# Turning the row maxima on TensorE: an ordinary product on 24 columns in place of the transpose mode on 128

## The chip, the cores and the metric

The kernel runs on one core of a Trainium2 chip. The metric is the device time of one execution in microseconds (us); lower is better. A core has a matrix engine (TensorE, "PE" in the profile, its weight loads "PEld"), a vector engine (VectorE, "DVE"), a scalar engine (ScalarE, "ACT"), a general engine (GpSimd, "POOL") and a queue engine (SyncE, "SP") that issues most DMAs.

## The reference

Two independent halves of the output, side by side. The left one is a causal attention with a memory over four segments, the right one a Fourier mixing of another input:

```python
B, S, D = x.shape                       # 1, 2048, 576
H = 32; Dh = D // H; N = 4; L = S // N  # heads of 18, segments of 512
...
for s in range(N):
    qs, ks, vs = q[:, :, s], k[:, :, s], v[:, :, s]
    logits = jnp.einsum("bhqd,bhkd->bhqk", qs, ks) * scale + mask
    p = _softmax(logits, axis=-1)
    a_dot = jnp.einsum("bhqk,bhkd->bhqd", p, vs)
    pq = phi(qs)
    num = jnp.einsum("bhld,bhde->bhle", pq, M)
    den = jnp.einsum("bhld,bhd->bhl", pq, z)[..., None] + 1e-6
    o = g * (num / den) + (1.0 - g) * a_dot
    ...
    M = M + jnp.einsum("bhld,bhle->bhde", phi(ks), vs)
    z = z + jnp.einsum("bhld->bhd", phi(ks))
return o @ wo
...
a = jnp.einsum("bsd,ed->bse", x, dft_hid_re)
b = jnp.einsum("bsd,ed->bse", x, dft_hid_im)
y = jnp.einsum("ts,bse->bte", dft_seq_re, a) - jnp.einsum("ts,bse->bte", dft_seq_im, b)
```

All inputs and the output are float32.

## The kernel before

The kernel writes the order of every engine's instructions out by hand. It has three stages. In the first, up to some 220 us, the projections are computed segment by segment, with the sums of the memory (`accumulate`, L363) and the look-ups in it. In the second, up to some 930 us, two streams are woven together: the dense products of the Fourier half (`hidden`, L622 to L627, and `sequence` over `product`, L577) and the attention. A loop over 64 steps and a tail (`attention`) issues the attention in eight slots a step; between the slots a generator (`dense`) fills in dense products in proportion to planned costs. The third stage is the product with `wo` (L84).

The attention works on groups `G` of four heads of one segment, 32 groups in all; a step takes two heads. Their softmax needs each query's largest logit. For the "even" two heads of a group it goes this way:

- `s_fill` computes scores with queries on partitions (`scores`, L738, into PSUM banks of tag `s`) and takes each row's minimum of the negated scores on VectorE (`smallest`, L744) into `NEGM`, eight columns: two heads by four blocks of 128 queries.
- `maxima` (L788 to L791, GpSimd) cuts these eight float32 columns into three bfloat16 parts each, 24 columns of the tile `mb`. There are two such tiles, and their other columns are zero from two memsets (L483) that run once, at the beginning of the second stage.
- `maxima_transpose` turns them: the 24 columns become 24 rows of 128 queries. TensorE does it in transpose mode on all 128 columns (L795), into a free part of the PSUM bank that the score product L815 has just filled (tag `t`). ScalarE copies 24 rows out (L797, tile `mt`), and two DMAs on SyncE's queue put them as three more rows under the queries in `qs`.
- One step later `t_fill` computes the scores a second time, with keys on partitions and with these three rows in the contraction (L812, L815, L820, L821), so that the maximum is already taken off. ScalarE takes the exponentials out of the bank (L824, L825).

The turn's place in the order is fixed: it follows L815 in `t_fill(n, 1)` of every even step, directly ahead of dense products or, three times, of score products. Only for group 0, where no `t_fill` runs yet, does it have a bank of its own (`trm`). Each bank is used again once the engine that reads it is done.

TensorE's weight loads and products are separate records in the profile. A product names its operands as `out<-moving,stationary`. An f32 product here carries its own load; a bf16 one has an instruction of its own for it.

Of the kernel before, what the change touches and what calls it, by code (L numbers as in the profile page):

```python
# [15 lines left out]
BF16 = mybir.dt.bfloat16  # L16
AF = mybir.ActivationFunctionType
# [6 lines left out]
P = 128  # L24
# [16 lines left out]
def infini_attention_and_fnet(ctx: ExitStack, tc: tile.TileContext, xT, wqk, w8, wv, wo, beta, xtT, cT, hT, out):  # L41
    nc = tc.nc
    act, dve, pool, pe = nc.scalar, nc.vector, nc.gpsimd, nc.tensor
# [25 lines left out]
    ident16 = const.tile([P, P], BF16, name="ident16")  # L69
# [18 lines left out]
    def later(n, fn, *a):  # L88
        due.setdefault(clock[0] + n, []).append((fn, a))
# [112 lines left out]
    for i in range(2):  # L202
        kn.append(tuple(sk.tile([P, D], F32R, name=f"kn{n}{i}") for n in "hl"))
        t = sk.tile([P, 2, H, 19], F32R, name=f"vn{i}")
# [3 lines left out]
    for i in range(3):  # L208
        t = sb.tile([P, H, 55], BF16, name=f"vs{i}")
# [258 lines left out]
    CAUSAL, NEGM, MB, OG = [], [], [], []  # L468

    def attention_tiles():  # L470
        t = sr.tile([P, L], F32, name="causal")
        CAUSAL.append(t)
        for i in range(2):
            NEGM.append(sr.tile([P, 8], F32, name=f"negm{i}"))
            MB.append(sr.tile([P, P], BF16, name=f"mb{i}"))

    def attention_constants():
        t = CAUSAL[0]
        pool.memset(t, 0.0)
        pool.affine_select(t[:, 384:], t[:, 384:], pattern=[[-1, P]], base=0, channel_multiplier=1,  # L480
                           compare_op=OP.is_ge, fill=LOWEST)
        for m in MB:
            pool.memset(m, 0.0)  # L483

    NG = 32

# [13 lines left out]
    for s in range(NSEG):  # L500
# [8 lines left out]
        for n, m in enumerate((0, 1, 2, 3, 8, 4, 5, 6, 7)):  # L509
            project_qk(s, m)  # L510
            tick()
            if not more and n in (5, 7):
                h_split(0, (n - 5) // 2)
            if s and n < (8 if more else 4):
                copy_parts(s - 1, 2 * n)
                copy_parts(s - 1, 2 * n + 1)
            if s in (1, 2) and n >= 4:
                load_x(s + 1, n - 4)
            if not more and n == 0:
                for k in range(5):  # L520
                    h_load(0, k)
            if not more and n == 4:
                p1k.close()
                sr = ctx.enter_context(tc.tile_pool(name="sb2r", bufs=1, side="right", reuse_waits="tile"))
                attention_tiles()
            if not more and n == 4:
                c_load(0)
                c_load(1)
                stacks(sr, 0)
                stack_load(0)  # L530
            if not more and n == 6:
                c_load(2)
        for j in range(4):
            project_v(s, j, lookup(s, j) if s else iter(()))
            tick()
            for k in ((0, 1), (2, 3), (4,), ())[j] if s == 0 else ():
                load_x(1, k)
            if more and j in (1, 2):
                split_x(s + 1, j - 1)
            if not more and j == 1:  # L540
                stacks(sr, 1)
            if not more and j == 2:
                attention_constants()
            if not more and j == 0:
                h_split(0, 2)
                h_split(0, 3)
            if not more and j == 1:
                h_split(0, 4)
                c_cut(0, dve)
                c_cut(1, dve)  # L550
            if not more and j in (1, 3):
                c_load(3 + j // 2)
            if more and j:
                accumulate(j - 1)
# [228 lines left out]
        nc.sync.dma_start_transpose(PT[n], hl.rearrange("p a c -> p (a c)"))  # L783

    def maxima(G):
        m, b = NEGM[G % 2].rearrange("p (h n) -> p h n", h=2), MB[G % 2][:, :24].rearrange("p (h c n) -> p c h n", h=2, c=3)
        r = sa.tile([P, 2, 4], F32, name="negx", bufs=2)
        pool.tensor_copy(b[:, 0], m)  # L788
        pool.tensor_tensor(r, m, b[:, 0], OP.subtract)
        pool.tensor_copy(b[:, 1], r)  # L790
        pool.tensor_tensor(b[:, 2], r, b[:, 1], OP.subtract)  # L791

    def maxima_transpose(G, o):
        t = o[:, 384:448].bitcast(BF16)
        pe.transpose(t, MB[G % 2], ident16)  # L795
        w = sa.tile([24, P], BF16, name="mt", bufs=2)
        act.activation(w, t[:24], AF.Copy)  # L797
        for h in range(2):
            later(1, dma, qs_bufs[G % 4][NPAIR:NPAIR + 3, 2 * h].rearrange("c (n t) -> c n t", n=4), w[12 * h:12 * h + 12])

    def t_fill(n, kind, maxima_of=None):
        G, h = divmod(n, 4)
        q, k = qs_bufs[G % 4][:NPAIR + 3, h], ks_bufs[G % 4][:NPAIR + 3, h]
        if kind == 0:
            PT[n] = (sa.tile([P, 1280], F16, name="phi", bufs=2), sa.tile([P, 1280], F16, name="plo", bufs=2),
                     sa.tile([P, 1280], F32, name="pf", bufs=3))
        hi, lo, f = PT[n]
        o = bank("t", [P, L], F32, "t")
        if kind == 0:
            for j in range(4):  # L810
                b = slice(j * P, (j + 1) * P)
                pe.matmul(o[:, b], k[:, b], q[:, b], start=True, stop=True)  # L812
            r, w = 0, 512
        elif kind == 1:
            pe.matmul(o[:, :384], k[:, :128], q[:, 128:], start=True, stop=True)  # L815
            if maxima_of is not None:
                maxima_transpose(maxima_of, o)
            r, w = 512, 384
        else:
            pe.matmul(o[:, 256:384], k[:, 256:384], q[:, 384:], start=True, stop=True)  # L820
            pe.matmul(o[:, :256], k[:, 128:256], q[:, 256:], start=True, stop=True)  # L821
            r, w = 896, 384
        if kind:
            act.activation(hi[:, r:r + w], o[:, :w], AF.Exp, bias=LIFT, scale=SCALE)  # L824
        act.activation(f[:, r:r + w], o[:, :w], AF.Exp, bias=LIFT, scale=SCALE)  # L825
# [89 lines left out]
    def attention():  # L915
        for p in range(NP + V_LAG):
# [28 lines left out]
            if G is not None and p < T_LAG:  # L945
                maxima_transpose(G, bank("trm", [P, L], F32, "t"))
# [11 lines left out]
            if p % 2 and p < NP:  # L958
                maxima(p // 2)
# [28 lines left out]
    for w in attention():  # L988
        tick()
        ta += w  # L990
        while td / total_d < ta / total_a:
            t = next(d, BREAK)
# [14 lines left out]
    for t in range(NT):  # L1007
# [3 lines left out]
        for h in range(2):  # L1011
            cs = slice(h * 288, h * 288 + 288)
            o = ps.tile([P, 288], F32, name="d", bufs=3)
# [53 lines left out]
```

## Time and profile before

| | |
|---|---|
| median of three runs | 1001.27 us (1000.71 to 1001.88) |
| profiled execution | 1002.62 us, of which the span of the core's instructions is 1000.9 us |
| mean granted TensorE clock | 0.998 |
| busy share of the span | TensorE 99%, its loads 92%, VectorE 75%, ScalarE 71%, GpSimd 64% |
| turns of the maxima | 32 products of 221 ns and 32 loads of 98 ns in the records, 32 copies of 250 ns |

The times of the engines' parts are those of one profiled execution. TensorE's products overlap: a record's duration reaches from a product's start to its modelled end, and the next one starts long before it. What a product costs is therefore read from starts, not from durations.

### The profile page before, as it was taken

What the parts mean: (1) busy time and instruction counts of PE and PEld (TensorE: products, weight loads), DVE (VectorE), ACT (ScalarE), POOL (GpSimd) and SP (SyncE); (2) the same over time, 40 slices, a digit from 0 to 9 for tenths busy, and PEclk for the clock granted to TensorE, in tenths of its full rate; (3) what the DMA queues carried; (4) which work ended last, traced back from release to release, by engine and by line L of the source; (5) the groups of instructions that cost most, each with busy time, mean ns of one, the idle gap of its engine ahead of it and who ended that gap; (6) DMA issues with size and microseconds to landing.
All of it is one profiled execution on the core that took longest, in us unless ns stands there. A gap on an engine that the chain in (4) does not pass through costs nothing.

```text
span 1000.9 us, 25591 instructions
## 1 busy us (share of the span) xinstructions
PE 990.0 (99%) x9294; PEld 925.6 (92%) x9294; DVE 752.7 (75%) x2052; ACT 712.3 (71%) x1680; POOL 635.9 (64%) x700
## 2 busy tenths in 40 slices
PE   9999999989999999999999999999999999999998
PEld 8989989889999999999999999999999999999998
DVE  6557667594678777878898888898888899998321
ACT  7757575653887787878778788877767777777243
POOL 2657576675767667666766776776767767767000
PEclk9999999999999999999999999999999999999999
DMA  7537456767588999899999987889999999989455
GB/s 248 185 117 252 178 176 244 233 231 217 143 186 211 219 240 227 203 236 220 249 220 238 218 218 191 180 203 233 226 227 213 233 237 247 248 188 200 127 150 139
DMA packets 305614, 208.92 MB, mean 209 GB/s; under 512 B 206288, under 2 KB 260432, under 8 KB 305488
## 3 DMA queue, kind: packets, MB, share of 16 engines
q1 hardware_dynamic: 305248, 207.15, 81.0%
q8 instruction: 73, 1.20, 0.5%
q14 instruction: 53, 0.43, 0.2%
q10 hardware_dynamic: 240, 0.14, 0.0%
HBM read 121.32 MB, written 57.93 MB: 179 GB/s over the span
## 4 chain that ended last, share of the span: by engine, by line
PE 85%; DVE 5%; ACT 4%; issue 2%; POOL 1%; DMA 1%; SPq 0%; POOLq 0%; DVEq 0%; ACTq 0%
PE d L577 38%; PE s L738 7%; PE d L84 6%; PE v L84 4%; PE pv L856 4%; PE qk L250 4%; PE d L622 3%; PE d L623 3%; PE d L624 3%; PE pv L857 2%; PE m L363 1%; PE t L812 1%; PE qk L84 1%; DMA craw<-cT 1%; DVE r L276 1%
## 5 line engine op out<-in xcount | busy, mean ns | idle before, releaser
L744 DVE CUSTOM_DVE_ANT_0 s<-s,causal 128x128 f32<-128x128 f32 (+3 forms) x512 | 249.7, 498 | 103.2 <-PE s L738 94.1
L456 POOL TENSOR_TENSOR clo<-craw,chi 128x512 fp32r<-128x512 f32 x158 | 216.8, 1372 | 100.0 <-ACT chi L451 73.1
L577 PE MATMUL d<-wide,chi 128*128 128x288 f32 x1408 | 266.2, 306 | 0.4 <-DVE y L647 0.4
L577 PEld LDWEIGHTS d<-wide,chi 128*128 128x128 f32 x1408 | 211.8, 189 | 3.2 <-issue 0.9
L577 PE MATMUL d<-wide,clo 128*128 128x288 f32 x704 | 177.5, 319 | 0.0
L778 POOL TENSOR_TENSOR hl<-pf,hl 128x768 f16<-128x768 f32 x64 | 112.9, 1764 | 68.6 <-ACT hl L774 55.3
L824 ACT ACTIVATE phi<-t 128x384 f16<-128x384 f32 x128 | 61.7, 482 | 103.4 <-PE t L821 103.3
L738 PE MATMUL s<-ks,qs 108*128 108x128 bf16 (+3 forms) x512 | 133.9, 304 | 1.3 <-ACT pf L767 0.8
L767 ACT ACTIVATE pf<-s,nb 128x128 f32<-128x128 f32 (+3 forms) x256 | 128.3, 527 | 6.2
L839 DVE TENSOR_TENSOR plo<-pf,phi 128x384 f16<-128x384 f32 (+1 forms) x128 | 126.4, 987 | 0.0
L577 PE MATMUL d<-ab,chi 128*128 128x288 f32 x640 | 126.0, 306 | 0.0
L577 PEld LDWEIGHTS d<-wide,clo 128*128 128x128 f32 x704 | 118.6, 189 | 1.6
L825 ACT ACTIVATE pf<-t 128x384 f32<-128x384 f32 (+1 forms) x192 | 99.5, 518 | 6.1 <-PE t L812 5.9
L451 ACT ACTIVATE chi<-craw 128x512 fp32r<-128x512 f32 x160 | 100.1, 626 | 4.1 <-DMA craw<-cT 2.2
L577 PEld LDWEIGHTS d<-ab,chi 128*128 128x128 f32 x640 | 98.5, 189 | 0.6
L774 ACT ACTIVATE hl<-pf 128x768 f16<-128x768 f32 (+1 forms) x128 | 87.4, 729 | 2.0
L622 PE MATMUL d<-wide,chi 128*128 128x288 f32 x256 | 84.8, 331 | 2.8 <-ACT xtail L453 2.8
L577 PE MATMUL d<-ab,clo 128*128 128x288 f32 x320 | 84.8, 314 | 0.0
L623 PE MATMUL d<-wide,chi 128*128 128x288 f32 x256 | 76.1, 297 | 0.0
L624 PE MATMUL d<-wide,clo 128*128 128x288 f32 x256 | 76.0, 297 | 0.0
L778 DVE TENSOR_TENSOR hl<-pf,hl 128x512 f16<-128x512 f32 x64 | 67.7, 1058 | 0.1
L839 POOL TENSOR_TENSOR plo<-pf,phi 128x384 f16<-128x384 f32 x64 | 59.4, 928 | 12.9 <-ACT pf L825 10.3
(214 smaller groups left out, 2500.0 us busy)
## 6 DMA issues: line engine op xcount, KB each, us to landing
craw<-cT SPq DMA_DIRECT2D x128, 256.0 KB
ks<-kd SPq DMA_DIRECT2D x32, 432.0 KB
qs<-qd SPq DMA_DIRECT2D x32, 432.0 KB
craw<-xtT SPq DMA_DIRECT2D x32, 320.0 KB
vd<-vs SPq DMA_DIRECT2D x16, 440.0 KB
vst<-vd SPq DMA_DIRECT2D x32, 220.0 KB
qd<-p SPq DMA_DIRECT2D x16, 384.0 KB
kd<-p SPq DMA_DIRECT2D x16, 384.0 KB
```

The lines of the kernel that those rows point to most:

```text
L84: pe.matmul(o, a, b, start=n == 0, stop=n == len(terms) - 1)
L451: act.activation(hi, raw[:, :4], AF.Copy)
L456: engine.tensor_tensor(lo, raw[:, :4], hi.bitcast(F32), OP.subtract)
L577: pe.matmul(o[h], a, b[:, h * 288:h * 288 + 288], start=start, stop=stop)
L622: pe.matmul(o, xh[:, k], wl[k][:, cs], start=k == 0, stop=False)
L623: pe.matmul(o, xh[:, k], wh[k][:, cs], start=False, stop=False)
L624: pe.matmul(o, xl[:, k], wh[k][:, cs], start=False, stop=False)
L738: pe.matmul(o[:, c:c + w], q[:, i * P:w], k[:, :w], start=True, stop=True)
L744: dve.tensor_tensor_reduce(o[:, c:c + w], o[:, c:c + w], CAUSAL[0][:, L - w:], scale=scale, scalar=-LOWEST, op0=OP.add, op1=OP.min, accum_ ...
L767: act.activation(f[:, FIRST_COL[i]:FIRST_COL[i] + w], o[:, c:c + w], AF.Exp, bias=nb[:, i:i + 1], scale=-1.0)
L778: engine.tensor_tensor(hl[:, 1, a:b], f[:, a:b], hl[:, 0, a:b], OP.subtract)
L839: (pool if kind == 2 else dve).tensor_tensor(lo[:, a:b], f[:, a:b], hi[:, a:b], OP.subtract)
```

## The change

The tiles `mb` have 24 columns instead of 128, so nothing is left to be zeroed and the two memsets go. The turn is an ordinary product with `mb` as stationary operand (24 columns) and the bfloat16 identity as moving operand (128 columns); it writes 24 rows of float32 instead of 128 rows of bfloat16, and ScalarE's copy reads float32. The order of the instructions on every engine is otherwise the same. In the built program the new load and product are set to a part of the array of 128 rows by 32 columns.

```diff
-            MB.append(sr.tile([P, P], BF16, name=f"mb{i}"))
+            MB.append(sr.tile([P, 24], BF16, name=f"mb{i}"))
...
-        for m in MB:
-            pool.memset(m, 0.0)
...
     def maxima(G):
-        m, b = NEGM[G % 2].rearrange("p (h n) -> p h n", h=2), MB[G % 2][:, :24].rearrange("p (h c n) -> p c h n", h=2, c=3)
+        m, b = NEGM[G % 2].rearrange("p (h n) -> p h n", h=2), MB[G % 2].rearrange("p (h c n) -> p c h n", h=2, c=3)
...
     def maxima_transpose(G, o):
-        t = o[:, 384:448].bitcast(BF16)
-        pe.transpose(t, MB[G % 2], ident16)
+        t = o[:24, 384:512]
+        pe.matmul(t, MB[G % 2], ident16, start=True, stop=True)
         w = sa.tile([24, P], BF16, name="mt", bufs=2)
-        act.activation(w, t[:24], AF.Copy)
+        act.activation(w, t, AF.Copy)
```

## The prediction

> **What bounds the kernel now.** I read the page first: the busy times, then the chain that ended last.
>
> ```profile
> span 1000.9 us, 25591 instructions
> PE 990.0 (99%) x9294; PEld 925.6 (92%) x9294; DVE 752.7 (75%) x2052; ACT 712.3 (71%) x1680; POOL 635.9 (64%) x700
> PE 85%; DVE 5%; ACT 4%; issue 2%; POOL 1%; DMA 1%; SPq 0%; POOLq 0%; DVEq 0%; ACTq 0%
> ```
>
> TensorE has work in 990.0 of 1000.9 us and carries 85% of the chain. The second view is who TensorE waited for.
>
> ```profile
> PE d L622 <- ACT xtail L453: 2.8, 1, 2.8
> ...
> PE s L738 <- ACT pf L767: 0.8, 1, 0.8
> ```
>
> Its longest wait is 2.8 us, once, where the projections give way to the attention; the first wait inside the attention stage that the list shows is 0.8 us. So an edit in the attention stage is worth what it takes from or adds to TensorE's own stream of instructions, and little else. The third view is the two tiles that the change touches, `mb` and `mt`.
>
> ```profile
> L795 PEld LDWEIGHTS <-mb x32: 95/98/101, 243.5 to 898.6; 128*128 128x128 bf16 x32
> L795 PE MATMUL t<-ident,mb x31: 219/221/222, 265.9 to 898.8; 128*128 128x128 bf16 x31
> L797 ACT ACTIVATE mt<-t x31: 247/250/252, 268.2 to 900.5; 24x128 bf16<-24x128 bf16 x31
> ```
>
> There are 32 of these turns (31 on tile `t`, one on `trm`), one load, one product and one copy each. A duration of 221 ns is not what a product costs, because products overlap: what counts is by how much later the next ones start. So the fourth view is the timeline around one turn, and around a step of the same kind that has none.
>
> ```profile
> 265.72 0.33 PE L815 MATMUL t<-qs,ks 111*128 111x384 bf16 x1
> 265.88 0.22 PE L795 MATMUL t<-ident,mb 128*128 128x128 bf16 x1
> 265.91 0.38 PE L622 MATMUL d<-wide,chi 128*128 128x288 f32 x1
> 266.12 0.29 PE L623 MATMUL d<-wide,chi 128*128 128x288 f32 x1
> 266.25 0.30 PE L624 MATMUL d<-wide,clo 128*128 128x288 f32 x1
> ```
>
> ```profile
> 590.24 0.40 PE L812 MATMUL t<-qs,ks 111*128 111x128 bf16 x4
> 590.48 0.33 PE L815 MATMUL t<-qs,ks 111*128 111x384 bf16 x1
> 590.50 0.43 PE L626 MATMUL d<-wide,xtail 128*128 128x288 f32 x1
> 590.77 0.29 PE L627 MATMUL d<-wide,xtail 128*128 128x288 f32 x1
> 590.90 0.29 PE L622 MATMUL d<-wide,chi 128*128 128x288 f32 x1
> ```
>
> From the start of L815 to the start of the second dense product behind it (L623 above, L627 below) it is 266.12 - 265.72 = 0.40 us with a turn and 590.77 - 590.48 = 0.29 us without; one product further 0.53 against 0.42. A turn costs TensorE 0.11 us, and all 32 cost 3.5 us, 0.35% of the span. That is the most that the change could save on this engine.
>
> **The turn itself.** Why 0.11 us, when four products of the same 128 moving columns (L812) start 0.24 / 4 = 0.06 us apart? The weight loads tell.
>
> ```profile
> 265.72 0.10 PEld L795 LDWEIGHTS <-mb 128*128 128x128 bf16 x1
> 265.88 0.19 PEld L622 LDWEIGHTS d<-wide,chi 128*128 128x128 f32 x1
> 265.99 0.19 PEld L623 LDWEIGHTS d<-wide,chi 128*128 128x128 f32 x1
> ```
>
> The load of `mb` starts with L815 and lies under it, since L815 keeps the array for 265.88 - 265.72 = 0.16 us. The next load, the f32 one of the dense product, starts only with the turn's product at 265.88, and the one behind it follows after 0.11 us. So the 0.11 us are the time of an f32 load that has only a short product above it; the turn's own streaming is inside. (Behind 3 of the 32, by the order of the program, stands a bf16 load of a score instead; the argument is the same there.) The changed kernel keeps the 128 moving columns, the place in the order, and the f32 load behind. The load of 24 columns instead of 128 is shorter, but it was hidden. Hence the main term: 32 x (0.11 - 0.11) = 0. Its cover is L815; if the `mb` load could not run under it, it would cost one load step, taken as the 0.06 us of the L812 row, 32 x 0.06 = 1.9 us.
>
> What the trace lacks is a bf16 product with 24 stationary columns. In the built program it runs on a part of the array, 128 rows by 32 columns, where its neighbours use 128 by 128; the array is switched twice at each turn. The nearest rows are the sums of the memory (L363), whose last piece has 64 stationary columns and uses 128 by 64.
>
> ```profile
> L363 PEld LDWEIGHTS m<-vn,knh x72: 138/188/194, 42.9 to 174.9; 128*128 128x128 f32 x60, 128*64 128x64 f32 x12
> ```
>
> ```profile
> 61.25 0.19 PEld L363 LDWEIGHTS m<-vn,knh 128*128 128x128 f32 x1
> 61.36 0.14 PEld L363 LDWEIGHTS m<-vn,knh 128*64 128x64 f32 x1
> 61.43 0.19 PEld L250 LDWEIGHTS qk<-xh,wide 128*128 128x128 f32 x1
> 61.54 0.19 PEld L250 LDWEIGHTS qk<-xl,wide 128*128 128x128 f32 x1
> ```
>
> ```profile
> 61.43 0.23 PE L363 MATMUL m<-vn,knh 128*64 128x152 f32 x1
> 61.50 0.43 PE L250 MATMUL qk<-xh,wide 128*128 128x512 f32 x1
> ```
>
> Into the narrow piece the loads are 61.36 - 61.25 = 0.11 us apart, as between full f32 loads (61.54 - 61.43 = 0.11); out of it 61.43 - 61.36 = 0.07 us, less, since 64 columns load faster. The full load of L250 starts at 61.43, with the narrow product and not after its 0.23 us. Neither edge shows a stop. I take 0 for the switch. Bounds: below, the whole of today's 0.11 us saved; above, a stop at both edges, priced under the rivals.
>
> The Trainium skill, "TensorEngine Tiling (Array Packing)", section Tiling Modes, speaks against this: "Changing tiling mode (not just tile) drains the TensorE". The rows at 61.36 and 61.43 do not show it for 64 columns; no row here tries 32. The skill's "TensorE: Matmul & The Clock Gate", section on weight-path modes, also says that the fast weight load needs 128 columns, so the new load would lose it.
>
> **The wait that goes.** The old product wrote 128 rows of which the copy read 24; the new one writes 24. So 30 loads of later scores (L738) lose a wait for TensorE's own counter, met some 80 products earlier. One such place (521.35) and one without the wait (510.92):
>
> ```profile
> 521.35 0.39 PE L738 MATMUL s<-ks,qs 108*128 108x512 bf16 x1
> 521.39 0.62 PE L577 MATMUL d<-ab,chi 128*128 128x288 f32 x2
> ```
>
> ```profile
> 510.92 0.39 PE L738 MATMUL s<-ks,qs 108*128 108x512 bf16 x1
> 510.96 0.62 PE L577 MATMUL d<-wide,clo 128*128 128x288 f32 x2
> ```
>
> The next product follows after 0.04 us in both. Worth: 0.
>
> **The copy on ScalarE** reads 128 f32 elements a row instead of bf16. Bounds from f32 copies out of PSUM:
>
> ```profile
> L405 ACT ACTIVATE nd<-look 128x133 f32<-128x133 f32 x12 | 3.4, 286 | 0.0
> ...
> L406 ACT ACTIVATE nd<-look 128x76 f32<-128x76 f32 x12 | 3.0, 246 | 0.0
> ```
>
> ```profile
> ACT phi L824 <- PE t L821: 103.3, 61, 3.6
> ```
>
> Between 246 ns for 76 and 286 ns for 133 elements, 128 give about 283 ns, against 250 now: 32 x 0.033 = 1.1 us more on ScalarE. Behind it in that queue stand the exponentials (L824, L825), and behind those the bank that TensorE refills. ScalarE then waits for TensorE, 103.3 us in all at L824, so I take 0; if none of that slack lay behind it, 1.1 us. A gain of as much is possible only if the bf16 read is the slower, which these rows exclude.
>
> **The two memsets** of `mb` on GpSimd go. They stand ahead of the 2.8 us wait:
>
> ```profile
> 221.06 0.42 DVE L458 TENSOR_TENSOR xtail<-craw,xtail 64x128 fp32r<-64x128 f32 x1
> 221.29 0.35 POOL L483 MEMSET mb<- 128x128 bf16 x2
> ```
>
> ```profile
> 224.20:228.70 4.50, 4.50 (x23) 4.28 (x24) 2.62 (x10) 0.41 (x1) 4.36 (x4) 0.62 0.51 167
> ```
>
> GpSimd's later work waits for ScalarE anyway. VectorE's L458 ends at 221.48, 0.19 us after the first memset began; if the two disturb each other, at most 0.19 us goes from the chain to the wait. I take half, 0.1 us.
>
> **Sum.** 0 + 0 + 0 - 0.1 us. The profiled execution took 1002.62 us (span 1000.9) and would become 1002.5; it lies 1.35 us above the median of the three runs, 1001.27, so the forecast for the median is 1001.2. Three runs spread over 1.2 us, so about 0.2%, 2.0 us, is what a measurement of this kernel can tell from no change.
>
> **Rivals.**
>
> Slower, by the switch: the array empties before it changes its split. At entry alone the load waits for L815's end (0.33 us) and takes 0.10, so the turn starts 0.43 us after L815 instead of 0.16: +0.27 x 32 = 8.6 us, 1009.9. At the exit alone the f32 load waits for the turn's 0.22 us: +7.0 us, 1008.3. Both, 15.7 us, 1017. It decides as soon as the stop exceeds 0.06 us a turn. For it: the array really is split otherwise. Against: L363. Chance 0.12. The rule quoted above is this rival.
>
> A little slower: the load loses only its place under L815, +1.9 us, 1003.2. For it: a load of this form is new here. Against: 0.16 us of cover. Chance 0.08.
>
> Faster: the exposed f32 load gets earlier, and a turn costs its 0.06 us of streaming: 32 x 0.05 = 1.6 us, 999.7; at most 3.5 us, 997.8. For it: the new load leaves most columns alone. Against: at 61.43 the full load still starts with the narrow product. Chance 0.06.
>
> Faster, at the seam: after the 2.8 us wait TensorE's granted clock is 0.62 for 4.5 us, a loss of 4.5 x 0.38 = 1.7 us. A wait shorter by up to 0.19 us may escape it: 999.4. Against: most of the wait stays. Chance 0.04.
>
> **How the numbers follow.** No measurable change has 0.70. The range 999.0 to 1004.0 takes in that case with the spread of runs, ScalarE's 1.1 us, the small loss and the seam, together 0.82; it leaves out the stops and the larger gain. Faster by over 0.2%: most of the 0.06, and part of the seam, 0.08. Slower: the stops, half of the small loss, some scatter, 0.20. Same: 0.72.
>
> **What would show it.** Right: 0.40 us from L815 to the second dense product behind a turn, as now; the load of 24 columns still starting with L815; the copy at some 283 ns; the same chain. Wrong: that distance at 0.46 (the small loss), at 0.6 or more (a stop), or at 0.35 and less (the gain); or a granted clock of 1 behind the seam.

## The result: slower by 0.8%, and the profile after

| | before | after |
|---|---|---|
| median | 1001.27 us | 1009.19 us (1008.76 to 1009.38) |
| profiled execution / its span | 1002.62 / 1000.9 us | 1009.38 / 1007.6 us |
| ratio of the times, 95% interval | | 1.0079 [1.0068, 1.009] |

The change costs 7.9 us. The forecast of 1001.2 us and its range up to 1004.0 are wrong; the rival "slower, by the switch", given 0.12, is what happened.

First the page of the changed kernel: span, busy times and the chain that ended last.

```profile
span 1007.6 us, 25589 instructions
...
PE 997.5 (99%) x9294; PEld 925.9 (92%) x9294; DVE 756.3 (75%) x2052; ACT 712.3 (71%) x1680; POOL 635.9 (63%) x698
...
PE 88%; DVE 5%; ACT 4%; issue 1%; POOL 1%; DMA 0%; SPq 0%; DVEq 0%; POOLq 0%; ACTq 0%
```

The number of TensorE's products is the same, yet it is busy 997.5 - 990.0 = 7.5 us longer. The loads, ScalarE and GpSimd have not moved; VectorE is busy 3.6 us longer, with the same 5% of the chain. TensorE's time without work fell from 1000.9 - 990.0 = 10.9 to 10.1 us, which is why the span grew by 6.7 and not by 7.5.

Next the timeline of TensorE's products around the same turn as in the prediction (start, duration, line; lines are two lower than before).

```profile
265.68 0.33 PE L813 MATMUL t<-qs,ks 111*128 111x384 bf16 x1
265.94 0.23 PE L793 MATMUL t<-ident,mb 128*24 128x128 bf16 x1
266.09 0.40 PE L620 MATMUL d<-wide,chi 128*128 128x288 f32 x1
266.33 0.29 PE L621 MATMUL d<-wide,chi 128*128 128x288 f32 x1
266.46 0.30 PE L622 MATMUL d<-wide,clo 128*128 128x288 f32 x1
```

From the score product to the second dense one it is 266.33 - 265.68 = 0.65 us; before it was 0.40. The turn's product starts 0.26 us after the score product instead of 0.16 (256 against 162 ns in the median of the turns: 0.09 lost at the entry), and the second dense one 0.39 after the turn instead of 0.24 (0.15 lost at the exit). Behind that, 266.46 - 266.33 = 0.13 is the ordinary step again. The timeline of the weight loads shows the same from the other side.

```profile
265.63 0.10 PEld L813 LDWEIGHTS <-ks 111*128 111x128 bf16 x1
265.93 0.09 PEld L793 LDWEIGHTS <-mb 128*24 128x24 bf16 x1 [0.21 <-issue]
266.09 0.19 PEld L620 LDWEIGHTS d<-wide,chi 128*128 128x128 f32 x1
266.20 0.19 PEld L621 LDWEIGHTS d<-wide,chi 128*128 128x128 f32 x1
```

Before, the load of `mb` started together with the score product (265.72 and 265.72) and lay under it. Now it starts 0.25 us behind it, after 0.21 us in which the load path stood still and waited for nothing that the profile shows ("issue"). The f32 load before started with the turn's product; now it starts 0.15 us after. The groups of the turn's line show that this is no single case:

```profile
L793 PEld LDWEIGHTS <-mb x32: 88/88/89, 243.6 to 905.2; 128*24 128x24 bf16 x32
L793 PE MATMUL t<-ident,mb x31: 226/226/227, 265.9 to 905.2; 128*24 128x128 bf16 x31
...
  issue: 6.6, 30
```

30 loads waited 6.6 us in all for "issue" (the other two are put down to a GpSimd instruction). Added up over all 32 turns, from starts in ns, the distance to the second product behind the turn grew by 7.6 us, against 7.9 measured: some 0.24 us at a turn ahead of dense products, 0.20 at the three ahead of score products. The product's own record is 226 ns against 221: the durations hardly show the loss, the starts do.

The three small terms: the copy on ScalarE, the wait at the seam and the clock behind it, from the groups, the timeline and the table of stretches.

```profile
L795 ACT ACTIVATE mt<-t 24x128 bf16<-24x128 f32 x31 | 7.7, 250 | 0.0
```

```profile
220.78 0.42 DVE L458 TENSOR_TENSOR xtail<-craw,xtail 64x128 fp32r<-64x128 f32 x1
```

```profile
224.20:228.70 4.50, 4.50 (x25) 4.20 (x24) 2.33 (x10) 0.41 (x1) 4.28 (x4) 0.62 0.55 174
```

The f32 copy takes the same 250 ns. VectorE's L458 takes 0.42 us without the memsets as with them, and the clock behind the seam is 0.62 as before.

### The profile page after: what moved, and what is told of

It is laid out like the page before. It is cut to its first block, busy times and chain, and to the rows that moved or that the text cites. A ratio compares the mean times of both kernels' runs of the same rounds, so it can differ in the third digit from the quotient of the medians.

```text
span 1007.6 us, 25589 instructions
## 1 busy us (share of the span) xinstructions
PE 997.5 (99%) x9294; PEld 925.9 (92%) x9294; DVE 756.3 (75%) x2052; ACT 712.3 (71%) x1680; POOL 635.9 (63%) x698
## 4 chain that ended last, share of the span: by engine, by line
PE 88%; DVE 5%; ACT 4%; issue 1%; POOL 1%; DMA 0%; SPq 0%; DVEq 0%; POOLq 0%; ACTq 0%
PE d L575 40%; PE s L736 7%; PE d L84 6%; PE pv L854 4%; PE v L84 4%; PE qk L250 4%; PE d L620 3%; PE d L621 3%; PE d L622 3%; PE pv L855 2%; PE t L810 1%; PE m L363 1%; PE qk L84 1%; PE t L813 1%; DVE r L276 1%
## 5 line engine op out<-in xcount | busy, mean ns | idle before, releaser
L776 DVE TENSOR_TENSOR hl<-pf,hl 128x512 f16<-128x512 f32 x64 | 71.2, 1113 | 0.1
```

What stands on the lines that cost most here:

```text
L776: engine.tensor_tensor(hl[:, 1, a:b], f[:, a:b], hl[:, 0, a:b], OP.subtract)
```

## The experiments

The line of inquiry: is it the split of the array (theory A), the ordinary product as such (B), or a load of fewer than 128 columns (C)? Then: at which products does the stop arise, and what is today's 0.11 us? Ratios are against the kernel before on the same chip.

**p128: an ordinary product on all 128 columns.**

```diff
 (against the kernel before)
-        t = o[:, 384:448].bitcast(BF16)
-        pe.transpose(t, MB[G % 2], ident16)
+        t = o[:, 384:512]
+        pe.matmul(t, MB[G % 2], ident16, start=True, stop=True)
```

> The ordinary product with all 128 padded columns as stationary operand; only the transpose mode is given up, the array stays 128 by 128. Theory A (the cost is the change of the array's split, to a narrow setting and back): no loss, 0.40 us from L815 to the second dense product, 1001 us as before. Theory B (the ordinary product in itself is slower than the transpose mode): 1009 us, 0.65 us. Theory C (a load of fewer than 128 columns cannot run ahead under the product before it): 1001 us.

1000.82 us, ratio 0.9997 [0.9987, 1.0006]: the same time. The timeline of the products:

```profile
266.00 0.33 PE L815 MATMUL t<-qs,ks 111*128 111x384 bf16 x1
266.17 0.22 PE L795 MATMUL t<-ident,mb 128*128 128x128 bf16 x1
266.20 0.38 PE L622 MATMUL d<-wide,chi 128*128 128x288 f32 x1
266.41 0.29 PE L623 MATMUL d<-wide,chi 128*128 128x288 f32 x1
```

266.41 - 266.00 = 0.41 us. Theory B falls: the ordinary product costs what the transpose mode cost.

**c96: 96 columns, which the program sets to the whole array.**

```diff
 (against the kernel before)
-            MB.append(sr.tile([P, P], BF16, name=f"mb{i}"))
+            MB.append(sr.tile([P, 96], BF16, name=f"mb{i}"))
...
-        t = o[:, 384:448].bitcast(BF16)
-        pe.transpose(t, MB[G % 2], ident16)
+        t = o[:96, 384:512]
+        pe.matmul(t, MB[G % 2], ident16, start=True, stop=True)
```

> The ordinary product with 96 stationary columns, which the program sets to the whole array of 128 by 128. Theory A (split): 1001 us, since nothing is switched. Theory C (short load): about 1009 us, the load of mb starting some 0.25 us after the score product before it instead of with it. This is the run that parts A from C.

1001.39 us, ratio 0.9999 [0.999, 1.0008]. The groups of its turn:

```profile
L795 PEld LDWEIGHTS <-mb x32: 120/123/135, 243.6 to 897.8; 128*96 128x96 bf16 x32
L795 PE MATMUL t<-ident,mb x31: 219/221/222, 265.9 to 897.9; 128*96 128x128 bf16 x31
...
  issue: 0.2, 1
```

The load of 96 columns is longer than that of 128 (123 against 98 ns), yet it runs ahead under the score product as before, as the timeline of one turn shows:

```profile
265.77 0.33 PE L815 MATMUL t<-qs,ks 111*128 111x384 bf16 x1
265.77 0.12 PEld L795 LDWEIGHTS <-mb 128*96 128x96 bf16 x1
...
266.18 0.29 PE L623 MATMUL d<-wide,chi 128*128 128x288 f32 x1
```

The load starts with the score product, and from it to the second dense one it is 266.18 - 265.77 = 0.41 us (in the median of the turns 409 ns, as in the kernel before). Theory C falls for a load of 96 columns. The longer load agrees with what the Trainium skill says in "TensorE: Matmul & The Clock Gate", section on weight-path perf modes: the fast weight load is on only with 128 columns.

**c64: 64 columns, set to 128 by 64** (the same edit with 64 in place of 96).

> The ordinary product with 64 stationary columns, set to 128 by 64. Theory A in its wide form (any narrow split stops the array): 1009 us, 0.65 us from the score product to the second dense one. Theory A in a narrow form (64 columns are free, as the sums of the memory seemed to show, and only 32 stop it): 1001 us. Theory C: 1009 us.

1008.68 us, ratio 1.0075 [1.006, 1.009]. The timeline of the products:

```profile
265.40 0.33 PE L815 MATMUL t<-qs,ks 111*128 111x384 bf16 x1
265.66 0.24 PE L795 MATMUL t<-ident,mb 128*64 128x128 bf16 x1
265.83 0.40 PE L622 MATMUL d<-wide,chi 128*128 128x288 f32 x1
266.07 0.29 PE L623 MATMUL d<-wide,chi 128*128 128x288 f32 x1
```

0.26 us at the entry as with 24 columns, 266.07 - 265.40 = 0.67 us in all. Between 96 and 64 columns the array's setting changes, and the loss is there: theory A in its wide form. (The setting follows the number of columns, so no run has 64 or 24 bf16 columns on the whole array.) So 64 columns are not free either, and the prediction's comparison with the 64-column sums of the memory misled. The groups of the turn's line:

```profile
L795 PEld LDWEIGHTS <-mb x32: 106/106/106, 243.3 to 905.3; 128*64 128x64 bf16 x32
L795 PE MATMUL t<-ident,mb x31: 243/243/243, 265.7 to 905.3; 128*64 128x128 bf16 x31
```

The load of 64 columns takes 106 ns against 88 for 24, and the step from the turn to the next product 173 ns against 156 (medians): 18 and 17 ns more. So part of what is lost behind the turn's start appears to be the load of `mb` itself, which no longer lies under the score product. How much of the exit is this load, and how much a second stop, no run here parts.

**t24: the transpose mode on 24 columns.**

```diff
 (against the changed kernel)
-        t = o[:24, 384:512]
-        pe.matmul(t, MB[G % 2], ident16, start=True, stop=True)
+        t = o[:24, 384:448].bitcast(BF16)
+        pe.transpose(t, MB[G % 2], ident16)
```

> The transpose mode kept, on 24 columns, set to 128 by 32, its output bf16. Theory A: 1009 us, as the changed kernel, since the split alone matters. Theory B (ordinary product): 1001 us. Theory C: 1009 us.

1008.87 us, ratio 1.0079 [1.0064, 1.0094], its groups:

```profile
L793 PEld LDWEIGHTS <-mb x32: 88/88/89, 243.0 to 904.7; 128*24 128x24 bf16 x32
...
  issue: 6.5, 30
```

The same 88 ns and nearly the same idle time before the loads as in the changed kernel (6.5 against 6.6 us). Of the change's two parts, the ordinary product alone costs nothing (p128) and the 24 columns alone cost all (t24).

**twice24: the narrow load and product issued twice in a row.**

```diff
 (against the changed kernel)
-        pe.matmul(t, MB[G % 2], ident16, start=True, stop=True)
+        for _ in range(2):
+            pe.matmul(t, MB[G % 2], ident16, start=True, stop=True)
```

> The changed kernel with its load and product on 24 columns issued twice in a row. Theory A (the stop is paid at each change of the split, not at each narrow product): one short step more per turn, 0.03 to 0.06 us, 32 of them 1 to 2 us above the changed kernel: 1010 to 1011 us. Rival (each narrow product stops by itself): 0.24 us more a turn, 1017 us.

1010.47 us, ratio 1.0092 [1.0072, 1.0113]: about 1.3 us above the changed kernel, whose median was taken in another series. In the timeline the second narrow product is merged with the first:

```profile
354.69 0.33 PE L814 MATMUL t<-qs,ks 111*128 111x384 bf16 x1
354.94 0.28 PE L794 MATMUL t<-ident,mb 128*24 128x128 bf16 x2
355.16 0.67 PE L575 MATMUL d<-wide,chi 128*128 128x288 f32 x3
```

The loads are merged in the same way:

```profile
354.94 0.10 PEld L794 LDWEIGHTS <-mb 128*24 128x24 bf16 x2 [0.21 <-issue]
```

The dense product starts 355.16 - 354.94 = 0.22 us after the first narrow one, against 0.16 with one (212 and 156 ns in the median): 0.06 us for the second product, the step of any short one, and not another 0.24. Both narrow loads lie within 0.10 us, so a narrow load behind a narrow product is not held up; theory C falls for 24 columns too. The loss is paid once a turn, where the setting changes and changes back, and not by each narrow product.

**f24: the 24 columns in f32r.**

```diff
 (against the changed kernel)
-            MB.append(sr.tile([P, 24], BF16, name=f"mb{i}"))
+            MB.append((sr.tile([P, 24], BF16, name=f"mb{i}"), sr.tile([P, 24], F32R, name=f"mr{i}")))
...
         pool.tensor_tensor(b[:, 2], r, b[:, 1], OP.subtract)
+        pool.tensor_copy(MB[G % 2][1], MB[G % 2][0])
...
-        pe.matmul(t, MB[G % 2], ident16, start=True, stop=True)
+        pe.matmul(t, MB[G % 2][1], identr, start=True, stop=True)
```

(`identr` is the identity in f32r; it takes the place of `ident16`.)

> The changed kernel with the 24 columns and the identity in f32r instead of bf16 (one more GpSimd copy a group), so that the product carries its own load as the sums of the memory do; still set to 128 by 32. Theory A1 (every product on a narrow split stops the array, and the memory's pieces had merely hidden it): 1009 us, 0.65 us from the score product to the second dense one. Theory A2 (the stop belongs to the separate bf16 load; an f32 product with its own load has none): 1001 us, 0.40 us.

1001.69 us, ratio 1.0002 [0.9993, 1.0011]: no loss. The timelines of its products and loads:

```profile
494.94 0.33 PE L814 MATMUL t<-qs,ks 111*128 111x384 bf16 x1
494.97 0.36 PE L794 MATMUL t<-identr,mr 128*24 128x128 f32 x1
495.17 0.61 PE L575 MATMUL d<-wide,chi 128*128 128x288 f32 x3
```

```profile
494.95 0.10 PEld L794 LDWEIGHTS t<-identr,mr 128*24 128x24 f32 x1
495.11 0.19 PEld L575 LDWEIGHTS d<-wide,chi 128*128 128x128 f32 x1
```

The narrow load starts 0.01 us after the score product, under it, as the whole-array load did. The program gives this product the same setting of 128 by 32, and its neighbours are the same; only the type differs, and with it that the product carries its own load. So theory A holds for the bf16 products of this kernel and not for its f32 ones (the result that theory A2 forecast). Whether an f32 product really runs split, or ignores the setting, and whether the type or the separate load decides, no run here tells.

**ahead128 and ahead24: the turn ahead of the score product L815.** In the kernel before (ahead128) and in the changed one (ahead24) the call was moved up:

```diff
+            if maxima_of is not None:
+                maxima_transpose(maxima_of, o)
             pe.matmul(o[:, :384], k[:, :128], q[:, 128:], start=True, stop=True)
-            if maxima_of is not None:
-                maxima_transpose(maxima_of, o)
```

> The kernel before with the turn, in transpose mode on 128 columns, put ahead of the score product of 384 columns. If the 0.11 us of a turn is the f32 load behind it, left bare by a short product, as the prediction says, the turn now costs only its own step of 0.06 us, and 32 of them save 1.5 us: 999.8 us, 0.35 us from the turn or the score product, whichever is first, to the second dense product plus the turn's step. Rival (the turn costs its 0.11 us wherever it stands): 1001.3 us.

> The changed kernel with the turn put ahead of the score product of 384 columns instead of behind it. Theory A: the two stops of some 0.09 us each stay, but the load behind the exit is now a short bf16 one and the f32 load behind lies under the 0.16 us score product: some 0.05 to 0.1 us a turn less, 1005.5 to 1007.5 us. Rival (the loss comes from the f32 load that follows a narrow product): back to 1001 us or below.

1048.92 us, ratio 1.0478 [1.0462, 1.0494], and 1053.68 us, ratio 1.0512 [1.049, 1.0535]. Both missed, and neither answers its question. TensorE's waits in ahead128 say why:

```profile
PE t L817 <- ACT mt L797: 40.1, 31, 2.7
```

The call also issues ScalarE's copy. Once it stands ahead of the score product, that product writes a bank which the copy still reads, so TensorE waits 31 times for ScalarE, 40.1 us in all. In ahead24 the same wait is 37.2 us. The mean granted clock of the profiled runs falls from 0.998 to 0.990 (ahead24: 0.988). At 1049 us, 0.8% would be some 8 us and cover the rest of ahead128; this is an estimate that no run tests. The edit moved two steps where one was meant.

**first128 and first24: only the product moved, the copy left behind L815.**

```diff
+            if maxima_of is not None:
+                turned = maxima_transpose(maxima_of, o)   # the product alone
             pe.matmul(o[:, :384], k[:, :128], q[:, 128:], start=True, stop=True)
             if maxima_of is not None:
-                maxima_transpose(maxima_of, o)
+                maxima_copy(maxima_of, turned)            # ScalarE's copy and the DMAs
```

> The kernel before (transpose mode, 128 columns) with the turn's product ahead of the score product of 384 columns and its copy left behind that one, so that the score product waits for no copy. If a turn's 0.11 us are the f32 load behind it, left bare by a short product, then the f32 load now starts with the score product and lies under its 0.16 us: 0.46 us from the last of the four products of 128 columns to the second dense one become 0.41, some 28 x 0.05 = 1.5 us, 999.8 us. Rival (a turn costs 0.11 us wherever it stands): 1001.3 us.

999.71 us, ratio 0.9987 [0.9978, 0.9996]: 1.4 us less than the kernel before (by the interval 0.4 to 2.2 us), and the fastest here. Timelines of its products and of its loads; L815 is here the line of the four products of 128 columns, and L820 that of the score product of 384:

```profile
352.11 0.40 PE L815 MATMUL t<-qs,ks 111*128 111x128 bf16 x4
352.35 0.22 PE L795 MATMUL t<-ident,mb 128*128 128x128 bf16 x1
352.41 0.33 PE L820 MATMUL t<-qs,ks 111*128 111x384 bf16 x1
352.44 0.70 PE L577 MATMUL d<-wide,chi 128*128 128x288 f32 x3
```

```profile
352.35 0.10 PEld L820 LDWEIGHTS <-ks 111*128 111x128 bf16 x1
352.41 0.49 PEld L577 LDWEIGHTS d<-wide,chi 128*128 128x128 f32 x3
```

The turn now costs 352.41 - 352.35 = 0.06 us, and the f32 load starts with the score product at 352.41 and lies under it. From the last of the four products to the second dense one it is 412 ns in the median, against 465 in the kernel before. So the prediction's reading of the 0.11 us, a bare f32 load, is borne out: where the load is covered, a turn costs 0.05 us less.

> The changed kernel with the turn's product in that same place, its copy left behind. If the stops belong to the change of the split: entry 0.09 us later than a whole-array load, exit 0.10 us later, and the f32 load covered: some 0.61 us from the last product of 128 columns to the second dense one, against 0.46 in the kernel before, 0.14 us a turn, 1005 to 1006 us. Rival (the loss comes from the f32 load that stands behind a narrow product): 1000 to 1001 us.

1006.16 us, ratio 1.0055 [1.0041, 1.0068], close to the forecast. The timelines of its products and of two loads (L813: the four products, L818: the score product):

```profile
354.55 0.40 PE L813 MATMUL t<-qs,ks 111*128 111x128 bf16 x4
354.88 0.23 PE L793 MATMUL t<-ident,mb 128*24 128x128 bf16 x1
355.03 0.34 PE L818 MATMUL t<-qs,ks 111*128 111x384 bf16 x1
355.07 0.69 PE L575 MATMUL d<-wide,chi 128*128 128x288 f32 x3
```

```profile
354.87 0.09 PEld L793 LDWEIGHTS <-mb 128*24 128x24 bf16 x1
355.03 0.10 PEld L818 LDWEIGHTS <-ks 111*128 111x128 bf16 x1
```

The turn starts 0.33 us after the first of the four products (0.24 in first128: 0.09 more), and the score product 159 ns after the turn in the median (60 in first128: 0.10 more). With bf16 products on both sides 0.09 us is lost at the entry and 0.10 at the exit, 0.2 us a turn; 32 turns make 6.4 us, which is the whole difference to first128 (1006.16 - 999.71 = 6.45). The f32 load behind a narrow product is not the source of the loss. The entry costs the same behind a product of 128 columns as behind one of 384. The exit is larger in the changed kernel, 0.15, and the starts suggest why: in both kernels the next load starts 0.16 us after the narrow one, but the score product then comes with its load instead of 0.06 us behind it, while an f32 load takes its step of 0.11 us either way.

## Why the prediction was wrong, point by point

**What bounds the kernel**: right. TensorE's 7.5 us more of work became 6.7 us more of span.

**The turn itself**: right as far as it goes. The 0.11 us are the f32 load (first128), the ordinary product takes the place of the transpose mode at no cost (p128), and a longer load that is covered costs nothing (c96). That the load of 24 columns would be covered ("it was hidden") failed together with the next step.

**The switch of the array**: this is the step that failed. "Neither edge shows a stop. I take 0 for the switch." The rows at 61.25 to 61.54 were read rightly; they were the wrong neighbours. They are f32 products with a load of their own, and the changed product is bf16 with a load instruction. c64, with the very 64 columns of those rows, loses time in bf16; f24, with the 24 columns of the change, does not in f32. In place of the 0 the runs show some 0.24 us a turn, 7.6 us over the 32: the load of `mb` starts 0.25 us behind the score product instead of with it, and the next load 0.16 us behind that one. The prediction named the difference in columns (64 or 32) as what the rows leave open, and passed over the difference in type that stands in the same rows. The rule of the Trainium skill ("TensorEngine Tiling (Array Packing)", Tiling Modes) that a change of the tiling mode drains TensorE agrees with the bf16 turns, which lose 0.09 us at the entry and 0.10 at the exit in first24; the f32 products of f24 do not show it.

**The price in the rival**: right in kind, too large in size. Entry 0.27 and exit 0.22 us were worked out from the records' durations (0.33, 0.10, 0.22); 0.09 and 0.15 were measured. The durations reach to modelled ends, as the front of this document says; a stop is shorter than they are. Both edges would have given 15.7 us, where the runs show 7.9. That one edge alone (8.6 or 7.0) comes near the total is chance: time is lost at both.

**The wait that goes**: no loss or gain from it is to be seen; c64, whose built program keeps this wait, takes 1008.68 us, and t24 and the changed kernel, which lose it, 1008.87 and 1009.19. It was not tried by itself. **The copy**: 250 ns, not 283; the interpolation between two other copies was wrong, and without effect on the time. **The memsets**: no gain; L458 took 0.42 us without them, so the 0.1 us was not there. **The seam**: the clock behind it stayed at 0.62.

**The chances**: the stop had a rule for it, and a single group of rows against it that differed in type. 0.12 was too little for that, and the range, which ended at 1004.0, left out exactly this case.

## What to carry to other kernels

When a row stands in for an operation that the trace lacks, list all that differs between them (shape, type, how the operand is loaded), and keep the cost open for each difference that no row covers. A narrow stationary operand is not cheaper on a busy TensorE if it sets the array differently from its neighbours: here padding to 128 columns was free, and 24 or 64 columns in bf16 cost 0.24 to 0.26 us a turn (24 columns in f32r cost nothing). A short product stood better here ahead of a longer one than ahead of an f32 load: moving only the turn's product saved 1.4 us, while moving its copy along cost 47.6 us.

## What the runs showed of the hardware that was not expected

- Between bf16 products with separate loads, a change of the array's split in this kernel costs some 0.09 us at the entry and 0.10 at the exit (first24). Behind the score product of 384 columns the profile lists it as idle time of the load path put down to "issue" (6.6 us over 30 turns, more than is lost, since part of it lies under that product); in first24, with 128 columns ahead, it lists only 0.2 us, once. The product's duration hardly shows it (226 against 221 ns).
- The same split on an f32r product showed no stop (ratio 1.0002). Why is open.
- A bf16 load of 96 columns took 123 ns, one of 128 columns 98 ns, one of 64 columns 106 and one of 24 columns 88 ns.
- ScalarE's copy of 24 rows of 128 out of PSUM took 250 ns from bf16 and from f32 alike.
